# Block-sorted attention feeding a four-expert layer: another order for the first batch's stages and another chain for its sort weights

## The chip, the cores and the metric

The kernel runs on one core of a Trainium2 chip. Its metric is device time in microseconds (us), the median of the runs. The core has five engines with a queue each: TensorE (PE; its weight loads are listed apart as PEld), VectorE (DVE), ScalarE (ACT), GpSimd (POOL) and SyncE (SP). Transfers are issued by the queues of SP, POOL and ACT and carried out by sixteen DMA engines. Times inside a profile are microseconds from the start of its span.

## What is computed

Attention with sorted blocks, and then a dense mixture of four experts on its output. For 4 batches and 8 heads, a sequence of 768 is cut into 8 blocks of 96. An 8 x 8 matrix per head, normalised five times over, mixes the blocks of keys and values:

```python
P = sort_net
for _ in range(5):
    P = P - np.max(P, axis=-1, keepdims=True)
    P = np.exp(P)
    P = P / (np.sum(P, axis=-1, keepdims=True) + 1e-09)
    P = P / (np.sum(P, axis=-2, keepdims=True) + 1e-09)
k_sorted = einsum('bhij,bhjcd->bhicd', P, k_blocks)      # the same for v
scores = scale * q_block @ k_sorted_block.T              # each block against its own sorted block
x = softmax(scores) @ v_sorted_block                     # 3072 tokens x 512
p = domain_probs / (domain_probs.sum(-1) + 1e-09)
out = sum(p[:, e] * (np.maximum(x @ w1[e], 0) @ w2[e]) for e in range(4))   # w1: 512 x 1024
```

## The kernel before

The order is written out by hand: each engine runs its instructions in the order in which the code emits them (the pools only decide which buffer a tile gets), and waits on semaphores. There is no scheduler.

**The head.** All work of batch 0 up to the second layer of expert 0 is a hand-made list at the end of the function. The sort weights of all 32 heads are normalised together, as 32 rows of 64 numbers: five passes of one exp on ScalarE and six small VectorE instructions (L273 to L288), beside 84 and then 30 warm-up matmuls (`warm`). The result is spread (L293, half on VectorE, half on GpSimd), eight small matmuls (`r_half`, L305) turn it into a column per block, and `build_PI0` (L316) multiplies it with a mask into mixing blocks. Heads are taken in two quarters `qd` (heads 0 to 3 and 4 to 7), output blocks in two halves `hf`, and queries in four pieces `qq`, two in each half. The stages of the head are: `h_q`, transposed queries; `mix_half` and `mixed`, the mix of keys or values, and its copies; `h_w`, values transposed; `h_s`, scores and their exp; `h_a`, attention and its division; `h_x`, transposes into `xT`, the input of the experts. `group0` (L661) is expert 0's first layer, here mostly in groups of 192 columns, cut into two parts and put between the stages; `second_layer0` (L696) its second layer; it scales its result by that expert's weight.

**Buffers.** PSUM has two pools, `psM` and `psA`, of two tiles each. A new tile waits for the last reader of the buffer that it takes over.

**Loads.** GpSimd's queue issues, in this order: queries of the first half (both quarters), keys and values of quarter 0 and of quarter 1, expert 0's `w1` in two parts; then, when the sort weights are spread, queries of the second half, expert 0's `w2`, and `w1` and `w2` of experts 1 to 3; then queries, values and keys of batch 1. SyncE's queue writes the normalised domain weights to memory and reads them back spread over all partitions (`load_p`, tile `pb`). A load waits in its queue for the landing of the one that stands eight before it.

**After the head** come `second_layer0(0)`; the first layers of experts 1 and 2 for tokens 0 to 255 (`chunk_first`, L768, evacuated by VectorE, L774); VectorE's sums of their results (`h_sums`) and of expert 1's second weights (`weight_sums`, L727); expert 0 for the second half (`first_layer0`, evacuated by ScalarE, L674, and `second_layer0(1)`); and then, in chunks of 256 tokens, the rest of batch 0, with the attention of the next batch put into its slots by `PLANS`. Each unit of work calls a slot when it is done; `next_stages` puts the remaining head stages into the first slots.

Of the kernel before, what the change touches and what calls it, by code (L numbers as in the profile page):

```python
# [17 lines left out]
def kernel(  # L18
# [20 lines left out]
    P = 128  # L39
# [35 lines left out]
    sn = const.tile([GH, NB, NB], F32, name="sn")  # L75
    nc.sync.dma_start(sn[:], sort_net.rearrange("b h i j -> (b h) i j"))

# [17 lines left out]
    q0 = Tt[3].rearrange("p a f x -> p (a f x)").rearrange("p (f h r d) -> p f h r d", f=2, h=4, r=R)  # L95

# [44 lines left out]
    def load_half_queries(hf):  # L141
        for qd in range(2):
            nc.gpsimd.dma_start(
                q0[ds(64 * qd, 64), hf].rearrange("p h r d -> p h (r d)"), half_queries(qd, hf)
            )

    dummy = Hflat[:, ds(2 * NFC * 2 * P, P)]
# [12 lines left out]
    load_half_queries(0)  # L160
# [7 lines left out]
    load_natural(0, "v", 1)  # L168
    load_w1(0, 2)
# [10 lines left out]
    )  # L180

# [18 lines left out]
    vo = arena[:, ds(4 * NW + NQ + 4 * 4 * P, R * 4 * VW)].rearrange("p (r h w) -> p r h w", r=R, h=4)  # L200

# [16 lines left out]

    def spread_weights():
# [13 lines left out]
        pbs[(0, 0)] = load_p(0, 0)  # L233
# [11 lines left out]
    def warm(n):  # L245
        ps = psM.tile([P, 4, P], F32, tag="ps", name=f"ps_w_{state['n']}")
        state["n"] += 1
        for m in range(n):
            nc.tensor.matmul(ps[:, m % 4, :], dummy, dummy, start=True, stop=True)
# [3 lines left out]
    def h_q(qd, hf, copy):  # L253

        ps = psa([P, 2, R, 64], F16, f"ps_q_{qd}_{hf}")
# [12 lines left out]
    sn16 = const.tile([GH, NB, NB, CP], F16, name="sn16")  # L268
    warm(84)
    p_steps = spread_weights()  # L270
    nc.gpsimd.tensor_copy(ident6, ident[0:R, 0:R])
    for it in range(5):
        nc.scalar.activation(sn[:], sn[:], AF.Exp, bias=0.0, scale=1.0)  # L273
        if it == 4:
            for qd in range(2):
                h_q(qd, 0, nc.scalar.copy)
            warm(30)
        nc.vector.tensor_reduce(srow[:], sn[:], AX.X, ALU.add)
        nc.vector.reciprocal(srow[:], srow[:])
        nc.vector.tensor_tensor(sn[:], sn[:], srow[:].broadcast_to([GH, NB, NB]), ALU.mult)  # L280
        nc.vector.tensor_reduce(scol[:], sn[:].rearrange("p i j -> p j i"), AX.X, ALU.add)
        nc.vector.reciprocal(scol[:], scol[:])
        if it < 4:
            nc.vector.tensor_tensor(
                sn[:], sn[:],
                scol[:].rearrange("p j o -> p o j").broadcast_to([GH, NB, NB]),
                ALU.mult,
            )  # L288
            if it:
                next(p_steps)  # L290

    for a, eng in enumerate((nc.vector, nc.gpsimd)):
        eng.tensor_tensor(  # L293
            sn16[:, ds(a * HB, HB)],
            sn[:, ds(a * HB, HB)].rearrange("g i (j o) -> g i j o", o=1).broadcast_to([GH, HB, NB, CP]),
            scol[:].rearrange("g j (i o) -> g i j o", i=1).broadcast_to([GH, HB, NB, CP]),
            ALU.mult,
        )

    ps_R = psM.tile([P, 2, 512], F32, tag="ps", name="ps_R")  # L300
    Rv = ps_R[:, :, 0:HB * GH].rearrange("p a (i g) -> p a i g", g=GH)

    def r_half(a):
        for i in range(HB):
            nc.tensor.matmul(  # L305
                Rv[:, a, i, :], sn16[:, a * HB + i, :, :].rearrange("g j c -> g (j c)"),
                ident[0:GH, 0:GH], start=True, stop=True,
            )

# [32 lines left out]
    r_half(0)  # L342
# [970 lines left out]
    for qd in range(2):  # L1313
        for nm in ("v", "k"):
            load_natural(1, nm, qd)
# [65 lines left out]
```

## Time and profile before

| | |
|---|---|
| runs | 363.74 us median of 3 (362.68, 363.74, 364.23) |
| profiled execution | 363.03 us, its span 361.3 us |
| granted TensorE clock | 0.999 |
| busy: PE, PEld | 353.7 us (98%), 315.4 us (87%) |
| busy: VectorE, ScalarE, GpSimd | 276.6 (77%), 173.7 (48%), 134.2 (37%) |
| instructions | 10846, 4621 of them matmuls |
| moved by DMA | 40.47 MB |

A line of the timeline gives start, length, engine, source line, operation, the tile written and the tiles read, sizes and count, and in brackets the engine's idle time before it with what ended it. A group of matmuls is drawn as one line. The chain that ended last is followed back from the last instruction. Stretches give busy time of each engine in a window. Busy PE is not PE at its peak, since matmuls overlap and their ends are modelled.

### The profile page before, as it was taken

How to read it: one execution, taken by the hardware profiler on the slowest of the kernel's cores; microseconds unless marked ns; L12 is line 12 of the kernel's file. 1: busy time of each engine (PE TensorE's matmuls, PEld its weight loads, DVE VectorE, ACT ScalarE, POOL GpSimd, SP SyncE). 2: the span in 40 equal slices, each digit the busy share in tenths (PEclk: the TensorE clock that was granted, in tenths of full speed). 3: DMA queues.
4: the chain of work that ended last, by engine and by line, in shares of the span. 5: the costliest groups of instructions: out<-in, count | busy, mean ns of one | idle time of the engine just before them, and what ended most of it. 6: DMA issues, size and time to landing. Idle time of an engine off the chain costs nothing.

```text
span 361.3 us, 10846 instructions
## 1 busy us (share of the span) xinstructions
PE 353.7 (98%) x4621; PEld 315.4 (87%) x4621; DVE 276.6 (77%) x561; ACT 173.7 (48%) x306; POOL 134.2 (37%) x148
## 2 busy tenths in 40 slices
PE   8799999999999999999999999999999999999996
PEld 8686867888888888888889999999999998999995
DVE  5654798779788677868878978867679679587694
ACT  2665340451434355368937257175283481571750
POOL 8873010655022330000626318147065082180470
PEclk9999999999999999999999999999999999999999
DMA  7999999999999999935994310110302103102101
GB/s 100 204 206 230 209 210 199 200 192 177 189 167 146 201 121 172 166 80 72 170 200 78 60 60 2 60 60 3 94 27 47 73 3 60 61 2 62 58 11 49
DMA packets 71820, 40.47 MB, mean 112 GB/s; under 512 B 40534, under 2 KB 66524, under 8 KB 71772
## 3 DMA queue, kind: packets, MB, share of 16 engines
q0 software_dynamic: 36560, 19.93, 42.7%
q1 hardware_dynamic: 35068, 19.79, 27.8%
q8 instruction: 36, 0.59, 0.7%
q14 instruction: 12, 0.10, 0.1%
q10 hardware_dynamic: 144, 0.07, 0.1%
HBM read 42.00 MB, written 6.34 MB: 134 GB/s over the span
## 4 chain that ended last, share of the span: by engine, by line
PE 89%; DMA 6%; POOL 1%; DVE 1%; SPq 1%; ACT 1%; issue 1%; DVEq 0%; ACTq 0%; POOLq 0%
PE ps_Q L1141 24%; PE ps_h L768 16%; PE ps_p L753 10%; PE ps_X L1038 10%; PE ps_Z L1038 7%; PE ps_Q L1038 7%; DMA w<-in_moe_w_dram 4%; PE ps_h L661 3%; PE ps_o L696 3%; PE ps_p L803 2%; DMA vs<-arena 2%; PE ps_a L441 2%; PE ps_s L406 1%; PE ps_v L354 1%; SPq L368 1%; PE ps_k L387 1%
## 5 line engine op out<-in xcount | busy, mean ns | idle before, releaser
L1051 POOL TENSOR_TENSOR Hb<-tmp,pb 128x512 f16<-128x512 f32 x40 | 50.8, 1276 | 84.3 <-ACT tmp L1050 83.0
L768 PE MATMUL ps_h<-xT,w 128*128 128x256 f16 x576 | 67.8, 273 | 0.0
L768 PEld LDWEIGHTS <-w 128*128 128x128 f16 x576 | 55.1, 98 | 7.3
L1141 PEld LDWEIGHTS <-Hb 128*128 128x128 f16 x576 | 53.7, 98 | 5.6
L774 DVE SCALAR_TENSOR_TENSOR Hb<-ps_h,pb 128x1024 f16<-128x1024 f32 x36 | 44.0, 1223 | 17.9 <-PE ps_h L768 17.7
L1038 PEld LDWEIGHTS <-w 128*128 128x128 f16 x864 | 52.4, 98 | 1.2 <-issue 0.3
L1141 PE MATMUL ps_Q<-w,Hb 128*128 128x256 f16 (+1 forms) x352 | 43.4, 268 | 0.0
L1038 PEld LDWEIGHTS <-arena 128*128 128x128 f16 x552 | 33.4, 98 | 0.1
L413 ACT ACTIVATE ET<-ps_s 96x768 f16<-96x768 f32 x24 | 18.1, 802 | 26.5 <-PE ps_s L406 26.2
L1038 PE MATMUL ps_X<-kT,arena 128*128 128x128 f16 x384 | 29.3, 219 | 0.0
L1058 ACT COPY ps_X<-ps_Z 128x512 f32<-128x512 f32 x27 | 15.4, 570 | 28.7 <-PE ps_Z L1038 28.3
L396 ACT CAST kT<-ps_k 64x384 f16<-64x384 f32 x48 | 22.7, 474 | 12.8 <-PE ps_k L387 11.8
L1074 DVE TENSOR_TENSOR tmp<-ps_Q,tmp 128x512 f32<-128x512 f32 x26 | 18.0, 692 | 14.1 <-ACT tmp L1073 9.9
L121 POOL DMA_DIRECT2D arena<-in_q_dram x24 | 19.9, 837 | 19.1 <-DMA qT<-arena 18.2
L739 DVE TENSOR_TENSOR Sb<-Hb 128x512 f16<-128x512 f16 x45 | 26.3, 608 | 0.9 <-POOL Hb L1051 0.8
L1141 PE MATMUL ps_Q<-T,Hb 128*128 128x256 f16 x224 | 26.7, 273 | 0.0
L1050 ACT ACTIVATE tmp<-tmp 128x512 f32<-128x512 f32 x40 | 25.4, 634 | 1.2 <-DVE tmp L1074 1.0
L753 PEld LDWEIGHTS <-Hb 128*128 128x128 f16 x232 | 21.9, 98 | 3.0
L1141 PEld LDWEIGHTS <-Sb 128*128 128x128 f16 x240 | 22.1, 98 | 2.3
L1065 ACT COPY tmp<-ps_X 128x512 f32<-128x512 f32 x26 | 15.2, 586 | 13.0 <-PE ps_X L1038 13.0
L1051 POOL TENSOR_TENSOR Hb<-tmp7x,pb 128x512 f16<-128x512 f32 x14 | 19.0, 1355 | 5.7 <-ACT tmp7x L1050 5.7
L1044 DVE SCALAR_TENSOR_TENSOR Hb<-ps_X,pb 128x512 f16<-128x512 f32 x27 | 18.5, 684 | 2.7 <-PE ps_X L1038 2.7
(205 smaller groups left out, 652.8 us busy)
## 6 DMA issues: line engine op xcount, KB each, us to landing
w<-in_moe_w_dram POOLq DMA_DIRECT2D x7, 1024.0 KB, 27.7
pb<-p_dram SPq DMA_DIRECT2D x12, 512.0 KB, 5.5
arena<-in_k_dram POOLq DMA_DIRECT2D x8, 384.0 KB, 9.0
arena<-in_v_dram POOLq DMA_DIRECT2D x8, 384.0 KB, 9.0
vs<-arena SPq DMA_DIRECT2D x36, 66.0 KB, 5.6
arena<-in_q_dram POOLq DMA_DIRECT2D x24, 96.0 KB, 7.5
out_dram<-ob SPq DMA_DIRECT2D x9, 256.0 KB, 2.0
out_dram<-oa SPq DMA_DIRECT2D x8, 256.0 KB, 2.3
```

The source lines that it names most:

```text
L121: nc.gpsimd.dma_start(t[:, h // 2, :, h % 2, :], q[b, h].rearrange("(t p) d -> p t d", p=P))
L396: nc.scalar.copy(kT[ds(D * hh, D), r], pk[ds(D * r, D), hh].rearrange("p a (i c) -> p a i c", c=CP),)
L413: nc.scalar.activation(ETs[2 * (pr % 2) + hh][:, 0:S].rearrange("c (a x) -> c a x", a=2), pss[hh][0:BLK, :, 0:HS], AF.Exp, bias=0.0, scale ...
L739: tt(sm[0], blk(0, 1), blk(1, 1), ALU.add)
L753: nc.tensor.matmul(ps, lhs(e, f), Ts[e][rhs][:, f, :], start=(first and e == es[0] and f == 0), stop=(done and e == es[-1] and f == KH - 1 ...
L768: nc.tensor.matmul(ps[:, f, :], w1sb[e][:, kc, ds((4 * g + f) * P, P)], xT[:, kc, ds(2 * c * P, 2 * P)], start=(kc == 0), stop=(kc == NKC ...
L774: nc.vector.scalar_tensor_tensor(out=Hb[:, e, ds(4 * g, 4), :], in0=ps[:], scalar=0.0, op0=ALU.max, in1=pb[:, ds(e, 1), :].broadcast_to([P ...
L1038: nc.tensor.matmul(dst[:, ds(f * P, P)], a[lhs][:, k, ds(f * P, P)], t[rhs][:, k, :], start=(first and f == 0 and k == 0), stop=(f == KH - ...
L1044: nc.vector.scalar_tensor_tensor(out=Hb[:, e, ds(i * KH, KH), ds(j * P, P)], in0=src.rearrange("p (f x) -> p f x", f=KH), scalar=0.0, op0= ...
L1050: nc.scalar.activation(src, src, AF.Relu, bias=0.0, scale=1.0)
L1051: nc.gpsimd.tensor_tensor(Hb[:, e, ds(i * KH, KH), ds(j * P, P)], src.rearrange("p (f x) -> p f x", f=KH), pb[:, ds(e, 1), ds(j * P, P)].b ...
L1141: nc.tensor.matmul(ps, lhs(e, f), Ts[e][rhs][:, f, part], start=(first and e == 0 and f == 0), stop=(e == E - 1 and f == KH - 1), skip_gro ...
```

## The change

1. The sort weights of batch 0 (8 heads, 64 rows) get a chain of their own. Two loads (SP and ACT queues) bring them in; VectorE transposes them; each pass is an exp on ScalarE with the column factor as its scale, a f32 matmul with a block mask for the row sums, a reciprocal, a product that also sums the columns, and a reciprocal. The spread result goes through one matmul to the blocks. The other 24 heads follow in `later_steps`, one step in each slot after the head.
2. On GpSimd's queue the quarters of the queries are parted, the masks are made before the last of the quarter-1 loads, `w1` of expert 0 goes out after the memsets, and the second block build stands ahead of the second-half queries and expert 0's `w2`.
3. The list of the head's stages is in another order; expert 0's first layer comes in groups of 384 columns, after both query pieces of the first half. Warm-ups are 256 or 512 columns wide instead of 128.
4. The domain weights are written out in the head's start, and `pb` is asked for behind them. Expert 1's first layer for tokens 256 to 511 (`homes` puts it into expert 0's place) is done ahead of expert 3's first layer for tokens 0 to 255, with domain weights of its own, loaded by `load_p_one`.
5. `PLANS` moves entries of batch 1's attention by two to four slots.

```diff
+    HJ = H * NB
+    sn0, snT = early(HJ, 32), early(HJ, 32)
+    blocks8 = early(HJ, HJ)
+    e0, r0, a0, c0, c0r = [early(HJ, n) for n in (NB, NB, NB, 1, 1)]
+    sel8 = early(HJ, NB)
+    sel, spread0 = [early(HJ, n, F16) for n in (P, HJ)]
...
+    for n, eng in enumerate((nc.sync, nc.scalar)):
+        eng.dma_start(
+            sn0[ds(32 * n, 32)].rearrange("i (h j) -> i h j", j=NB),
+            bass.AP(tensor=sort_net.tensor, offset=n * H // 2 * NB * NB, ap=[[NB, 32], [NB * NB, H // 2], [1, NB]]),
+        )
+    nc.sync.dma_start(sn[:], sort_net.rearrange("b h i j -> (b h) i j"))
...
-    load_half_queries(0)
+    load_half_queries(0, [0])
+
+    nc.gpsimd.memset(blocks8, 1.0)
+    for base, m in ((0, 1), (NB - 1, -1)):
+        nc.gpsimd.affine_select(
+            out=blocks8, in_=blocks8, compare_op=ALU.is_ge, fill=0.0, base=base,
+            pattern=[[-m * NB, H], [0, NB]], channel_multiplier=m,
+        )
     load_natural(0, "k", 0)
...
     load_natural(0, "v", 0)
     load_natural(0, "k", 1)
-    load_natural(0, "v", 1)
-    load_w1(0, 2)
...
+    load_half_queries(0, [1])
+    load_natural(0, "v", 1)
...
+    load_w1(0, 2)
...
+    def load_p_one(b, c, e):
+
+        pb = Tt[3].rearrange("p a f x -> p (a f x)")[:, 0:4 * P].bitcast(F32)
+        nc.sync.dma_start(pb, p_dram[ds(e, 1), ds(b * S + 2 * c * P, 2 * P)].broadcast_to([P, 2 * P]))
         return pb
...
-        pbs[(0, 0)] = load_p(0, 0)
...
-    warm(84)
...
+    warm(7, 256)
+    nc.vector.transpose(snT, sn0)
     nc.gpsimd.tensor_copy(ident6, ident[0:R, 0:R])
+    now, scale = snT[:, 0:NB], 1.0
     for it in range(5):
-        nc.scalar.activation(sn[:], sn[:], AF.Exp, bias=0.0, scale=1.0)
-        if it == 4:
-            for qd in range(2):
-                h_q(qd, 0, nc.scalar.copy)
-            warm(30)
-        nc.vector.tensor_reduce(srow[:], sn[:], AX.X, ALU.add)
-        nc.vector.reciprocal(srow[:], srow[:])
-        nc.vector.tensor_tensor(sn[:], sn[:], srow[:].broadcast_to([GH, NB, NB]), ALU.mult)
-        nc.vector.tensor_reduce(scol[:], sn[:].rearrange("p i j -> p j i"), AX.X, ALU.add)
-        nc.vector.reciprocal(scol[:], scol[:])
+        nc.scalar.activation(e0, now, AF.Exp, bias=0.0, scale=scale)
+        sums = ps_c[0:HJ, 0, ds(it * NB, NB)]
+        nc.tensor.matmul(sums, blocks8, e0, start=True, stop=True)
         if it < 4:
-            nc.vector.tensor_tensor(
-                sn[:], sn[:],
-                scol[:].rearrange("p j o -> p o j").broadcast_to([GH, NB, NB]),
+            warm((4, 5, 7, 7)[it], 256)
+        else:
+            h_q(0, 0, nc.scalar.copy)
+        nc.vector.reciprocal(r0, sums)
+        nc.vector.scalar_tensor_tensor(
+            out=a0, in0=e0, scalar=1.0, op0=ALU.mult, in1=r0, op1=ALU.mult, accum_out=c0
+        )
+        nc.vector.reciprocal(c0r, c0)
+        now, scale = a0, c0r
+        if it in (1, 2):
+            pick_rows(it - 1)
+        if 0 < it < 4:
+            next(p_steps)
...
+    nc.vector.scalar_tensor_tensor(
+        out=spread0.rearrange("p (g i) -> p g i", i=NB), in0=a0.rearrange("p (o i) -> p o i", o=1).broadcast_to([HJ, H, NB]),
+        scalar=c0r, op0=ALU.mult, in1=blocks8.rearrange("p (g i) -> p g i", i=NB), op1=ALU.mult,
+    )
+    ps_R0 = psM.tile([P, 2, 512], F32, tag="ps", name="ps_R0")
+    R0 = ps_R0[:, 0, 0:HJ].rearrange("p (g i) -> p g i", i=NB)
+    nc.tensor.matmul(ps_R0[:, 0, 0:HJ], sel, spread0, start=True, stop=True)
+
+    def later_steps():
+
+        gp = nc.gpsimd
+        gp.memset(sn16[ds(GH, GH)], 0.0)
+        gp.memset(sn16[ds(2 * GH, 2 * GH)], 0.0)
+        for it in range(5):
+            nc.scalar.activation(sn[:], sn[:], AF.Exp, bias=0.0, scale=1.0)
+            yield
+            nc.vector.tensor_reduce(srow[:], sn[:], AX.X, ALU.add)
+            nc.vector.reciprocal(srow[:], srow[:])
+            gp.tensor_tensor(sn[:], sn[:], srow[:].broadcast_to([GH, NB, NB]), ALU.mult)
+            yield
+            nc.vector.tensor_reduce(scol[:], sn[:].rearrange("p i j -> p j i"), AX.X, ALU.add)
+            nc.vector.reciprocal(scol[:], scol[:])
+            if it < 4:
+                gp.tensor_tensor(
+                    sn[:], sn[:], scol[:].rearrange("p j o -> p o j").broadcast_to([GH, NB, NB]), ALU.mult,
+                )
+            yield
+        for a in range(2):
+            gp.tensor_tensor(
+                sn16[0:GH, ds(a * HB, HB)],
+                sn[:, ds(a * HB, HB)].rearrange("g i (j o) -> g i j o", o=1).broadcast_to([GH, HB, NB, CP]),
+                scol[:].rearrange("g j (i o) -> g i j o", i=1).broadcast_to([GH, HB, NB, CP]),
                 ALU.mult,
             )
-            if it:
-                next(p_steps)
-
-    for a, eng in enumerate((nc.vector, nc.gpsimd)):
-        eng.tensor_tensor(
-            sn16[:, ds(a * HB, HB)],
-            sn[:, ds(a * HB, HB)].rearrange("g i (j o) -> g i j o", o=1).broadcast_to([GH, HB, NB, CP]),
-            scol[:].rearrange("g j (i o) -> g i j o", i=1).broadcast_to([GH, HB, NB, CP]),
-            ALU.mult,
-        )
-
-    ps_R = psM.tile([P, 2, 512], F32, tag="ps", name="ps_R")
-    Rv = ps_R[:, :, 0:HB * GH].rearrange("p a (i g) -> p a i g", g=GH)
-
-    def r_half(a):
-        for i in range(HB):
+        for qd in range(2):
+            for nm in ("v", "k"):
+                load_natural(1, nm, qd)
+        for _ in range(3):
+            yield
+        ps = psa([P, 2, 512], F32, "ps_R")
+        Rv = ps[:, 0, 0:NB * GH].rearrange("p (i g) -> p i g", g=GH)
+        for i in range(NB):
             nc.tensor.matmul(
-                Rv[:, a, i, :], sn16[:, a * HB + i, :, :].rearrange("g j c -> g (j c)"),
-                ident[0:GH, 0:GH], start=True, stop=True,
-            )
-
+                Rv[:, i, :], sn16[:, i, :, :].rearrange("g j c -> g (j c)"), ident[:, 0:GH], start=True, stop=True,
+            )
+        nc.scalar.copy(Rs[:, H:GH, :].rearrange("p g i -> p i g"), Rv[:, :, H:GH])
+        builds(1)
...
-    r_half(0)
     for h0 in range(0, H, 4):
-        build_PI0(nc.vector, 0, h0, 4, Rv[:, 0, :, ds(h0, 4)].rearrange("p i g -> p g i"))
+        build_PI0(nc.vector, 0, h0, 4, R0[:, ds(h0, 4), 0:HB])
+    nc.scalar.copy(Rs[:, 0:H, :], R0)
+    build_PI0(nc.gpsimd, 1, 0, H, Rs[:, 0:H, HB:NB])
+    load_half_queries(1)
+    load_w2(0)
...
+    next(p_steps)
+    tile2 = lambda pool, nm: pool([P, 2, 512], F32, f"ps_{nm}")
+    mk0 = mix_half("k", 0, 0, psm, 2)
     mixed("k", 0, mk0, 0, 2, act)
+    mixed("k", 0, mk0, 2, 2, act)
     mv0 = mix_half("v", 0, 0, psa)
     mixed("v", 0, mv0, 0, 2, vec)
+    mixed("v", 0, mv0, 2, 2, vec)
     h_s(0, 0)
-    r_half(1)
-    mixed("k", 0, mk0, 2, 2, act)
-    vec(Rs.rearrange("p g (a i) -> p a g i", a=2), Rv.rearrange("p a i g -> p a g i"))
-    load_half_queries(1)
-    load_w2(0)
-    build_PI0(nc.gpsimd, 1, 0, H, Rs[:, 0:H, HB:NB])
+    ps_s01 = tile2(psm, "s01")
+    h_s(0, 1, ps_s01)
     h_w(0, vec, 0, 2, tails[("v", 0, 0)])
-    mixed("v", 0, mv0, 2, 2, vec)
     mk1 = mix_half("k", 1, 0, psm)
+    w01 = h_w(0, None, 2, 2, side(ps_s01))
+    w01(vec)
+    ps_a00 = tile2(psa, "a00")
+    h_a(0, 0, ps_a00)
     mixed("k", 1, mk1, 0, 2, act)
+    ps_a01 = tile2(psa, "a01")
+    h_a(0, 1, ps_a01)
+    h_q(1, 0, act, psm)
     mixed("k", 1, mk1, 2, 2, act)
-    ps_a00, ps_s10 = [psa([P, 2, 512], F32, f"ps_{n}") for n in ("a00", "s10")]
-    h_a(0, 0, ps_a00)
+    h_x(0, None, [0], ps_a00)
     mv1 = mix_half("v", 1, 0, psm)
-    mixed("v", 1, mv1, 0, 2, act)
+    ps_s10 = tile2(psm, "s10")
     h_s(1, 0, ps_s10)
-    ps_s01 = psm([P, 2, 512], F32, "ps_s01")
-    w01 = h_w(0, None, 2, 2, side(ps_s01))
-    h_x(0, act, [0], ps_a00)
+    copies.pop(0)(act)
+    mixed("v", 1, mv1, 0, 2, vec)
+    h_x(1, None, [0], ps_a01)
+    ps_s11 = tile2(psa, "s11")
+    h_s(1, 1, ps_s11)
+    copies.pop(0)(act)
+    mixed("v", 1, mv1, 2, 2, vec)
     h_w(1, vec, 0, 2, tails[("v", 1, 0)])
-    mixed("v", 1, mv1, 2, 2, act)
-    h_s(0, 1, ps_s01)
-    w01(act)
-    ps_a10 = psa([P, 2, 512], F32, "ps_a10")
-    keep_warm(ps_a10[:, 0, 0:P], 4)
+    w11 = h_w(1, None, 2, 2, side(ps_s11))
+    w11(vec)
+    h_k(0, 1, act, psm)
+    ps_a10 = tile2(psa, "a10")
+    keep_warm(ps_a10[:, 0, :], 1)
     h_a(1, 0, ps_a10)
-    next(p_steps)
-    group0(0, 1, 0, [0, 1])
-    ps_a01 = psa([P, 2, 512], F32, "ps_a01")
-    w11 = h_w(1, None, 2, 2, side(ps_a01))
+    ps_a11 = tile2(psa, "a11")
+    h_a(1, 1, ps_a11)
     h_x(0, act, [1], ps_a10)
-    h_a(0, 1, ps_a01)
-    w11(vec)
-    group0(0, 1, 1, [0, 1])
-    ps_s11 = psa([P, 2, 512], F32, "ps_s11")
-    h_s(1, 1, ps_s11)
-    evacuate00 = group0(0, 1, 0, [2, 3], True)
-    h_x(1, act, [0], ps_a01)
-    evacuate00()
-    group0(0, 1, 1, [2, 3])
-    h_a(1, 1, ps_s11)
-    h_k(0, 1, act)
-    group0(1, 1, 0, [0, 1])
-    h_x(1, vec, [1], ps_s11)
-    group0(1, 1, 1, [0, 1])
+    group0(0, 2, 0, [0, 1])
+    group0(0, 2, 1, [0, 1])
+    h_x(1, act, [1], ps_a11)
+    group0(0, 2, 0, [2, 3])
+    h_v(0, 1, vec)
+    group0(0, 2, 1, [2, 3])
     h_k(1, 1, vec)
-    group0(1, 1, 0, [2, 3])
-    group0(1, 1, 1, [2, 3])
+    group0(0, 2, 2)
+    h_v(1, 1, vec)
+    h_w(0, vec)
+    h_q(0, 1, vec)
+    group0(0, 2, 3)
+    h_w(1, vec)
+    h_q(1, 1, vec)
...
-    builds(1)
+    load_queries(1, range(2))
+    others = later_steps()
...
     def next_stages():
+        next(others, None)
         if later:
             for f, *args in later.pop(0):
                 f(*args)
 
-    h_v(0, 1, act)
-    h_q(0, 1, vec)
     second_layer0(0, next_stages)
-    load_queries(1, range(2))
-    for qd in range(2):
-        for nm in ("v", "k"):
-            load_natural(1, nm, qd)
+    pbs[(0, 0)] = load_p(0, 0)
+    pb_1 = load_p_one(0, 1, 1)
     chunk_first(0, 0, [1, 2], 1, next_stages)
     h_sums(1, 4)
     for w in range(1, 5):
...
     all_sums(1, nc.vector)
     first_layer0(2, 2, next_stages)
     sums2 = weight_sums(2, nc.vector)
-    second_layer0(1, lambda: next(sums2, None))
+
+    def with_sums():
+        next_stages()
+        next(sums2, None)
+
+    second_layer0(1, with_sums)
     sums0 = weight_sums(0, nc.vector)
+    homes[1] = 0
+    chunk_first(0, 1, [1], 1, next_stages, lambda e: pb_1.rearrange("p (o x) -> p o x", o=1))
+    homes.clear()
```

## The prediction

> Times are us from the span's start unless said otherwise.
>
> **What bounds the kernel now.** I read the page's chain first, then busy time by stretches, then the timeline of the head and of the stretch around 50. The chain:
>
> ```profile
> PE 89%; DMA 6%; POOL 1%; DVE 1%; SPq 1%; ACT 1%; issue 1%; DVEq 0%; ACTq 0%; POOLq 0%
> ```
>
> TensorE sets the end; only its idle time and its own work count. By stretches (columns: us; busy PE, PEld, DVE, ACT, POOL; clock; DMA share; GB/s):
>
> ```profile
> 0.00:12.00 12.00, 9.66 (x166) 9.32 (x166) 7.44 (x34) 3.93 (x8) 9.41 (x29) 1.00 0.90 123
> 12.00:19.50 7.50, 6.00 (x172) 5.04 (x168) 4.62 (x11) 5.25 (x11) 6.56 (x10) 1.00 1.20 209
> 19.50:28.00 8.50, 8.43 (x166) 7.70 (x168) 4.06 (x9) 5.13 (x10) 6.95 (x8) 1.00 1.26 208
> ...
> 47.00:57.00 10.00, 9.99 (x55) 5.18 (x53) 9.74 (x18) 3.25 (x4) 0.74 (x1) 1.00 1.18 209
> ```
>
> The first 12 us are the sort chain under warm-up matmuls. 12 to 19.5 holds 1.5 us of PE idle, 19.5 to 28 nearly none. From 47 to 57 VectorE is as full as PE. In the head's timeline these rows give the anchors:
>
> ```profile
> 12.66 0.57 PE L483 MATMUL ps_mk<-Sb,arena 128*64 128x64 f16 x24
> 14.19 0.81 ACT L544 ACTIVATE ET<-ps_s 96x768 f16<-96x768 f32 x1 [0.44 <-PE ps_s L538]
> 16.13 0.57 PE L483 MATMUL ps_mv<-Sb,arena 128*64 128x64 f16 x24 [0.35 <-DMA arena<-in_v_dram]
> 19.57 0.83 PE L661 MATMUL ps_h<-xT,w 128*128 128x192 f16 x8 [0.83 <-DMA w<-in_moe_w_dram]
> 28.78 1.04 PE L696 MATMUL ps_o<-w,Hb 128*128 128x512 f16 x4
> ```
>
> The first key mix starts at 12.66, the second layer of expert 0 at 28.78. Two loads are waited for (values 16.13, w1 19.57); w2_0, issued at 13.89 and 14.8 us under way, lands at 28.7, just in time. Around 50:
>
> ```profile
> 50.33 0.69 DVE L727 TENSOR_TENSOR T<-w 128x1024 f16<-128x1024 f16 x1
> ...
> 52.50 0.69 DVE L727 TENSOR_TENSOR T<-w,T 128x1024 f16<-128x1024 f16 x1
> 53.11 0.68 DVE L727 TENSOR_TENSOR T<-w 128x1024 f16<-128x1024 f16 x1
> ```
>
> ```profile
> 50.85 0.81 ACT L674 ACTIVATE Hb<-ps_h 128x768 f16<-128x768 f32 x1 [0.55 <-PE ps_h L661]
> 52.09 0.81 ACT L674 ACTIVATE Hb<-ps_h 128x768 f16<-128x768 f32 x1 [0.43 <-PE ps_h L661]
> ```
>
> VectorE runs without a gap from 46.72 to 58 and is behind PE: expert 1's weight sums end at 53.1, when PE (second layer from 51.90) is already six matmuls in. ScalarE delivers the last hidden group at 52.9, just before it is read.
>
> **The skill.** "TensorE: Matmul & The Clock Gate", section on the array's architecture, calls ScalarE and VectorE strict FIFO: a waiting instruction holds all behind it. The trace agrees: a hidden group whose matmuls ended at 22.74 was evacuated only at 23.33, behind a copy at 22.95. The same page (What's actually happening) says the clock opens after about 3.4 us of activity; here matmul spacing halves near 5.5, after 4.4 us of warm-ups. "DMA: Bandwidth & Descriptors" (Issuing engines are not separate DMA queues) says all queues share the engines; the pb load issued at 26.29 took 11.7 us against a median of 5.5.
>
> **The change, part by part.**
> *Sort chain.* A pass takes 1.76 now (exps at 4.27, 6.04, 7.80). New pass: exp 0.26, f32 matmul 0.35 (nearest row: the f32 transpose, weights 0.13 + 0.22), reciprocal 0.19, product with running sum 0.25, reciprocal 0.19, handovers 0.3 (0.04 to 0.11 each in the trace) = 1.54. Bounds: 1.35 with a shorter matmul, 1.75 if the 256-column warm-ups ahead of it still run at the slow clock. The first exp starts at 2.85 (data at 2.5 as now, though in 256 short rows from two queues; ScalarE issues one, 0.4, and loads its table, 1.28, till then; one 32-block transpose 0.2 to 0.3, which no row shows). Five passes end at 10.55; product 0.25, matmul 0.3, first block build 0.37, handovers 0.15: key mix at 11.6 (10.8 to 12.3), 1.1 earlier than 12.66. The sums of the domain weights and the selector (0.16 to 0.28 each) fit into VectorE's wait of about 0.7 per pass.
>
> *Head order.* From the key mix, m, the new order is one thread through ScalarE, because the second half's query copy moves from 9.7 (idle ScalarE) into the middle. Durations from this trace: mix 0.57, two key copies 0.96, two exps 1.62, handover and the copy of R 0.2: m+3.35. The second value transpose writes into the score tile and so waits for that exp: transpose 0.39, copy 0.42, attention 0.41, query transposes 0.56, query copy 0.73, handovers 0.35: m+6.2. Key copy 0.48, scores 0.35, exp 0.81, xT copy 0.48 (the next score tile reuses its bank), scores 0.34, exp 0.81, value transposes 0.39, handovers 0.35: m+10.2. Mix 0.5, warm-up 0.22, attention 0.41, reciprocal and product 0.89, transposes 0.34, handovers 0.15: m+12.7. Four then four 384-column matmuls (0.163 each, from 32 in 5.2): 1.3 covers the other xT; its transposes and copy 0.85: m+14.8. What is left is PE work: 24 such matmuls 3.9, three mixes 1.5, two value transposes 0.9, two query transposes 1.0, waits for copies 0.3: m+22.4 = 34.0. Now the second layer starts at 28.78 but has 1.9 of that still to do (one mix, one query half, two value transposes at 0.46 to 0.5), so the like point is 30.7: 3.3 late. The 384-column form saves about 0.6 against the eight groups of 192 (0.66 to 0.83 each); that is inside. I take 3.0, for hops counted twice; bounds 0 (PE is never held, only w2_0's landing) and 4.5 (cold PE in addition).
>
> *Loads.* On GpSimd's queue the block mask (about 0.9, nearest rows 0.27 and 0.30) and then the small masks and memsets come before later issues: w1's two go out near 10 instead of 6.27, and w2_0 behind the second block build near 15 instead of 13.89. The queue is then still moving keys and values, which land till 16.1, so both are hidden by that backlog; without it each would cost its delay, 1 to 4. Bytes ahead of w1 and w2_0 are the same; keys of the second half land about 1 earlier, queries near 14, before ScalarE asks for them. The weights of the first 768 tokens and pb now leave at about 11 and 17 instead of 19.96 and 26.29; pb's 512 KB at 205 GB/s are 2.5, of which w2_0 already bore 0.5: it lands at about 30.7, under the 34.0 of PE, hidden (cost 1 to 2 if PE were early). pb for one expert, 128 KB, 0.6, is hidden by 5 us of later slack. The SyncE queue's query transpose now stands behind it, but its own data land near 62 either way.
>
> *The other 24 heads' chain* is moved into slots of the second layer and what follows: five exps on ScalarE, 20 small VectorE instructions (0.19 to 0.26), ten GpSimd products. Up to 46 VectorE has room; one pair sits before the product that the last xT transposes need (they started at 44.32 as soon as it ended): 0.4. The fourth and fifth pass sit behind expert 1's weight sums on the full VectorE, and the fifth exp sits on ScalarE ahead of the last hidden group's evacuation. From 53.1: reduce and reciprocal 0.45, GpSimd product 0.3 (nearest: 128x64 0.35, 128x32 0.24), reduce and reciprocal 0.5, product 0.3, exp 0.26, evacuation 0.81, handovers 0.25: 56.0. PE needs that group at 51.90 + 6 x 0.216 = 53.2. Stall 2.8; bounds 2.3 (products at 0.15) and 3.4. Behind it wait VectorE's two last ops, then the output scaling (57.3 to 58.0), which PE needs at 58.2: nothing more. The products sn16 and four loads of batch 1 wait on GpSimd too, to about 62; the values then land by 66 to 70, read near 72.
>
> *Moved at no price:* R for the other heads, 8 small matmuls, 0.3 more in a full stretch (before, in a head with gaps). Expert 1's layer ahead: 32 matmuls (3.5) change place; it gives expert 3's loads 3.5 more, which PE, late already, does not need. PLANS shifts: the slots lost are those of that expert; PE idle from 57 to 187 is under 0.4 now, so nothing is won and up to 1 could be lost.
>
> Sum: 3.0 + 2.8 + 0.4 + 0.3 = 6.5. The profiled execution took 363.03 (span 361.3): 369.5. The runs' median is 0.7 above it: about 370.
>
> **Rivals.** *Only one of the two costs appears* (+2.5 to +4, 366 to 368): for it, PE could fill the thread better than I count, as it does from 19.5 on now. *Nothing is felt* (within 0.5%): PE held only by w2_0 at 30.7, and the fifth exp in time; against it the full VectorE. *Faster:* the head is paced by loads alone. Then the second layer starts with w2_0; if pb does not delay it (28.7), that is 2.0 early: 361.7, at best 360. It decides if the thread from the key mix takes under 19 us, not 22.4, and the fifth exp's group stalls PE by less than the gain. For it: two DMA waits in the head now. *Slow clock:* the warm-ups have gaps; if the clock stays at half until the mixes, passes take 1.75 and the mixes 1 to 2 more: 372 to 374.
>
> **How the numbers follow.** Both costs 0.46, one of them 0.25, nothing felt 0.10, faster 0.11, slow clock on top 0.08. 0.5% is 1.8 us, about what a measurement can tell. Faster 0.11, same 0.10, slower 0.79. Likeliest 370 (its own range 367.5 to 372.5); the range 363 to 373 leaves out the faster case and the worst of the slow clock.
>
> **What would show it.** Key mix near 11.6 (right), second layer near 34 with ScalarE between its tiles all the way (right), or near 30 with a wait for w (wrong). In the second layer of the second half a PE wait of 2 to 3 us on ScalarE, with the small exp waiting on GpSimd (right). Without both, the prediction is wrong.

## The result, and the profile after

The changed kernel takes 377.05 us (median of 4 runs, 375.30 to 378.22), the kernel before 363.57 (362.68 to 364.23): ratio 1.0369, 95% interval 1.0322 to 1.0415. It is slower by 13.5 us where 6.4 were forecast, and lies above the forecast range. The profiled execution took 377.06, its span 375.3, 14.0 longer than before.

The chain of work that ended last, of the changed kernel:

```profile
PE 84%; DVE 7%; DMA 4%; ACT 2%; issue 1%; SPq 1%; POOL 0%; DVEq 0%; ACTq 0%; POOLq 0%
```

TensorE lost five points of the chain, and VectorE won six. Busy time by stretches, columns as before (us; busy PE, PEld, DVE, ACT, POOL; clock; DMA share; GB/s):

```profile
0.00:12.00 12.00, 9.36 (x74) 5.60 (x75) 5.02 (x30) 3.49 (x7) 9.22 (x31) 1.00 0.89 125
12.00:19.50 7.50, 5.46 (x176) 4.70 (x176) 4.91 (x12) 4.96 (x10) 6.30 (x10) 0.98 1.22 209
19.50:28.00 8.50, 7.16 (x73) 4.87 (x73) 2.54 (x6) 2.85 (x6) 2.92 (x4) 0.50 1.25 210
...
57.00:71.00 14.00, 11.40 (x67) 6.11 (x65) 10.45 (x21) 3.03 (x5) 8.22 (x11) 0.88 0.79 103
```

The news is in the clock column. From 19.5 to 28 TensorE runs at half clock, where it had 1.00 before; from 57 to 71 it idles for 2.6 and has half clock again for a part. In the trace's record of the clock, these stretches run from 19.25 to 29.49 and from 63.62 to 67.04. The record begins only when the clock first opens, at 9.0 here and at 5.4 in the kernel before; ahead of that the column reads 1.00, although the matmuls are spaced as at half clock (seven warm-ups of 256 columns take 1.68 from 6.67 on, and seven take 1.13 from 8.59 on). The anchors of the head, in the timeline:

```profile
11.91 0.57 PE L564 MATMUL ps_mk<-Sb,arena 128*64 128x64 f16 x24
17.74 0.67 PE L564 MATMUL ps_mv<-Sb,arena 128*64 128x64 f16 x24 [0.60 <-ACT Sb L297]
19.96 0.51 PE L619 MATMUL ps_s<-Sb,kT 64*128 64x96 f16 x8 [0.99 <-ACT xT L665]
25.02 2.76 PE L746 MATMUL ps_h<-xT,w 128*128 128x384 f16 x8
37.42 1.04 PE L781 MATMUL ps_o<-w,Hb 128*128 128x512 f16 x4
```

The key mix starts at 11.91. TensorE then waits for ScalarE's copies (the query copy at 17.7, the xT copy at 20), and eight matmuls of 384 columns take 2.76, 0.33 each, where one took 0.163 before. The second layer of expert 0 starts at 37.42. And around 60:

```profile
58.79 1.46 PE L781 MATMUL ps_o<-w,Hb 128*128 128x512 f16 x6
61.84 0.26 ACT L354 ACTIVATE sn<-sn 32x64 f32<-32x64 f32 x1 [3.29 <-POOL sn L363]
62.01 0.78 ACT L759 ACTIVATE Hb<-ps_h 128x768 f16<-128x768 f32 x1
62.85 4.88 PE L781 MATMUL ps_o<-w,Hb 128*128 128x512 f16 x14 [2.60 <-ACT Hb L759]
67.56 0.36 PE L382 MATMUL ps_R<-ident,sn 128*128 128x32 f16 x8
```

The fifth exponential of the later chain waits for GpSimd till 61.84 and holds the last hidden group's evacuation behind it; TensorE waits 2.60. The 14 matmuls that follow take 4.7, and 3.0 at the full clock (0.216 each).

Start of like work in both kernels (us):

| | before | after | later by |
|---|---|---|---|
| first key mix | 12.66 | 11.91 | -0.75 |
| first layers of experts 1 and 2 (all head work of TensorE's first half done) | 37.97 | 44.78 | 6.8 |
| expert 0, first layer, second half of the tokens | 46.52 | 53.41 | 6.9 |
| expert 0, second layer, second half | 51.90 | 58.79 | 6.9 |
| the first layer after it | 57.08 | 68.63 | 11.6 |
| end of the span | 361.3 | 375.3 | 14.0 |

So 6.8 are lost in the head, 4.7 in the second layer of the second half, 2.4 behind it.

### The profile page after: what moved, and what is told of

It is laid out like the page before. It is cut to its first block, busy times and chain, and to the rows that moved or that the text cites. A ratio compares the mean times of both kernels' runs of the same rounds, so it can differ in the third digit from the quotient of the medians.

```text
span 375.3 us, 10682 instructions
## 1 busy us (share of the span) xinstructions
PE 359.2 (96%) x4507; PEld 311.9 (83%) x4507; DVE 281.2 (75%) x579; ACT 173.1 (46%) x308; POOL 140.2 (37%) x163
## 4 chain that ended last, share of the span: by engine, by line
PE 84%; DVE 7%; DMA 4%; ACT 2%; issue 1%; SPq 1%; POOL 0%; DVEq 0%; ACTq 0%; POOLq 0%
PE ps_Q L1229 23%; PE ps_h L856 15%; PE ps_X L1126 9%; PE ps_p L840 8%; PE ps_Q L1126 6%; PE ps_Z L1126 6%; PE ps_o L781 3%; PE ps_p L891 2%; DMA vs<-arena 2%; PE ps_h L746 2%; DMA w<-arena 2%; PE ps_a L522 1%; PE ps_s L487 1%; PE ps_warm L283 1%; PE ps_v L435 1%
## 5 line engine op out<-in xcount | busy, mean ns | idle before, releaser
L862 DVE SCALAR_TENSOR_TENSOR Hb<-ps_h,pb 128x1024 f16<-128x1024 f32 x34 | 41.5, 1223 | 16.9 <-PE ps_h L856 16.7
L826 DVE TENSOR_TENSOR Sb<-Hb 128x512 f16<-128x512 f16 x45 | 27.6, 637 | 0.0
```

What stands on the lines that cost most here:

```text
L826: tt(sm[0], blk(0, 1), blk(1, 1), ALU.add)
L862: nc.vector.scalar_tensor_tensor(out=Hb[:, homes.get(e, e), ds(4 * g, 4), :], in0=ps[:], scalar=0.0, op0=ALU.max, in1=weights(e).broadcast ...
```

## The experiments

Each ran beside the kernel before on the same chip; the ratio is to those runs. The changed kernel itself stands at 1.0369.

### The head: does idle TensorE time close the clock gate?

*c1_head_warm*, the changed kernel with warm-ups in two waits of the head:

```diff
     h_x(0, None, [0], ps_a00)
+    keep_warm(ps_a00[:, 1, :], 3)
...
     h_x(1, None, [0], ps_a01)
+    keep_warm(ps_a01[:, 1, :], 4)
```

> The changed kernel with seven more 512-column warm-up matmuls: three behind the first tokens' transposes (0.6 us of idle there, near 17.1) and four behind the second tokens' transposes (1.0 of idle, near 19). Theory that the two idle stretches close the clock gate: the granted clock stays at 1.00 from 12 to 30, the matmuls between 19.5 and 29 run at 0.163 per 384 columns and not 0.32, the second layer of expert 0 starts at about 34.0 and not 37.5, and the whole takes 377.0 - 3.5 = 373.5. Rival, the head is held by the thread through ScalarE alone and the half clock only fills waits: the clock stays at 1.00, the second layer starts no more than 1 earlier, 376 to 377. Second rival, the gate closes for another reason than idle time: clock and time as in the changed kernel, or 0.5 longer.

Measured: 375.54, ratio 1.0347 (1.0304 to 1.0390). Its stretches and its second layer:

```profile
12.00:19.50 7.50, 6.56 (x182) 5.00 (x181) 4.86 (x13) 4.40 (x9) 5.87 (x9) 1.00 1.22 206
19.50:28.00 8.50, 6.49 (x107) 4.18 (x105) 3.11 (x9) 4.44 (x8) 3.33 (x4) 1.00 1.27 220
```

```profile
24.40 1.47 PE L746 MATMUL ps_h<-xT,w 128*128 128x384 f16 x8
34.97 1.04 PE L781 MATMUL ps_o<-w,Hb 128*128 128x512 f16 x4
```

The clock stays at 1.00, eight 384-column matmuls take 1.47 and not 2.76. From the key mix (12.39 in this execution) to the second layer it is 22.6, where the changed kernel takes 25.5: the half clock cost 2.9 in that execution, and the thread without it is nearly the forecast's 22.4. TensorE is 2.5 earlier at the second layer and 2.8 at the end. The medians are only 1.5 apart, since the runs of this kernel spread from 374.4 to 377.3 (what spreads them is taken up below), so the size is read from the trace, not from the total. All profiled executions with the new head, of this run and of those below, agree. The eight without these warm-ups (the changed kernel, c2, c3, d1, d2, d3, e2 and f3) went to half clock in the head for 6.8 to 13.7 us and took 25.1 to 27.7 for this thread; the three with them (c1, e3 and f2) never did, and took 22.6. In d2 the clock had first opened at the same time as in c1, 10.5, so the moment of opening is not what spared c1.

*c4_old_head*: the changed kernel with the list of head stages (and the first slots) of the kernel before, the query copy of quarter 1 behind the key copies.

> The changed kernel with the head stages of the kernel before: their order, the groups of 192 columns, the value mixes and query transposes of the second half left to the second layer's slots. The short sort chain, the loads, the wider warm-ups, the later chain and expert 1 ahead stay as changed. Theory that the new order of stages costs the head 6.8 of its lateness: the second layer starts at about 28.8 - 0.8 = 28.0 to 29, 377.0 - 6.8 = 370.2, with the stall of 2.6 near 55. Rival, the loads (w2 of expert 0 behind the second block build) or the queries' later load hold the old order too: the second layer starts at 31 or later, 373 or more.

Measured: 370.75, ratio 1.0234 (1.0176 to 1.0292), 6.3 under the changed kernel; nearly all that the table gives to the head. In its profiled execution, the slowest of the four at 374.8, the rival showed as well: TensorE waited 2.37 for expert 0's second weights, till 32.61. This execution had half clock three times, for 3.4 each. Two of the others (371.3 and 370.2) were granted 1.000 on average, so in them no half clock followed the stall near 60, which this program has too.

*f3_more_warm*: `warm((5, 6, 10, 12)[it], 256)` in the sort chain, for 4, 5, 7, 7.

> The changed kernel with 5, 6, 10 and 12 warm-up matmuls behind the row sums of the first four passes and not 4, 5, 7 and 7, so that TensorE has hardly a gap in the sort chain. Theory that the small row-sum matmuls and gaps keep the clock gate shut until 9 to 15: matmul spacing halves by 9 in every pass order, the key mix starts at 11.6 to 12.0, and the head is as before behind it; 376.5. Rival, the opening only depends on when matmuls began, and the added warm-ups delay each row sum by up to 0.3: key mix at 12.5 or later, 377 to 378.

Measured: 378.01, ratio 1.0387 (1.0329 to 1.0444), key mix at 12.81. The theory falls: more warm-ups delay the chain and do not bring the full clock sooner (it opens at 9.04, for 9.01 in the changed kernel). In the other profiled executions with the changed chain the key mix started between 11.8 and 12.7, and but for f1, whose passes were slower, it follows the opening of the clock: 11.8 to 11.9 where the clock opened at 8.2 to 9.0, 12.1 to 12.4 for 9.8 to 10.5, and 12.7 where it opened only at 14.7 to 16.4, behind the mix. With warm-ups without a break it opened at 5.4 (the kernel before) and 5.9 (e4). Why it opens so differently under one and the same chain is not shown; the last section has what the record of the clock says.

### The second layer: is it the exponential, and what does the half clock add?

*c3_stall_warm*, warm-ups put into the stall itself:

```diff
                 if fc == KH - 1:
                     slot()
+                if (hf, t, fc) == (1, 0, 5):
+                    keep_warm(po[:, 1, :], 12)
```

> The changed kernel with twelve 512-column warm-up matmuls (2.6 us) put into the stall of the second layer, ahead of the matmul that waits. The stall itself stays. Theory that the idle stretch closes the clock gate for the next 3.5 us: 14 matmuls behind it take 3.0 and not 4.9, 377.0 - 1.8 = 375.2. Rival, the clock falls for another reason (the heavy matmuls before it): no change, 377.

Measured: 375.02, ratio 1.0342 (1.0303 to 1.0381).

```profile
59.87 2.75 PE L550 MATMUL ps_o<-Hb 128*128 128x512 f16 x12
62.64 3.19 PE L781 MATMUL ps_o<-w,Hb 128*128 128x512 f16 x14
```

From the first of the 14 matmuls behind the stall to the matmuls of R (the eight small ones that turn the other heads' sort weights into columns, at 65.67 here) it is 3.0 and not 4.7. In the changed kernel's execution the wait of 2.6 costs 1.7 more than its own length, by the clock alone.

*c2_exp5_after*: `next_stages` skips the chain once, in its 13th call, so that the fifth exponential stands behind the last evacuation.

> The changed kernel with one slot left out of the later sort chain, so that its fifth exponential stands behind the last hidden group of tokens 768 to 1535 on ScalarE, and not ahead of it. Theory (the stall of the fourth step, and the half clock that follows it): no wait of 2.6 in the second layer, no half clock from 63.5 to 67 (1.75), together 4.35: 372.7. Rival, the stall is only moved: the matmuls of R and the scaled outputs come late instead, since the fifth pass now ends about 1 later, and the time is 375 to 377.

Measured: 376.09, ratio 1.0346 (1.0301 to 1.0390). The rival is right. TensorE no longer waits for ScalarE, but 1.4 for the scaled outputs (VectorE) and, in the middle of R's matmuls, 1.2 for a product of GpSimd that they read. No half clock follows these waits. From the start of the second half to the next first layer it is 8.5, for 9.8 in the changed kernel and 5.2 before. (Its head ran longer at half clock, till about 35, so the total says little.)

### Taking the chain out of the way, and a wait that takes its place

*d1_two_passes* (`for it in (0, 4)`: three of the five passes of the other 24 heads left out, which computes something else, to see the place without them) and *d2_early_chain*, all five passes but three steps in two slots:

```diff
     def next_stages():
+        held["n"] += 1
         next(others, None)
+        if held["n"] < 10 and held["n"] % 2:
+            next(others, None)
```

> The changed kernel, but the other 24 heads get two sort passes and not five (three are left out, so this computes something else); every step of that chain then stands nine slots earlier. Theory that the late fifth exponential and what hangs on it (R, the half clock) is the loss around 60: no wait of 2.6, no half clock behind it, the stretch from the first matmul of the second layer's second half to the next first layer takes 5.2 to 5.5 and not 9.8, and batch 1's loads leave near 55 and not 66. 377.0 - 4.4 = 372.6; and if the late loads of batch 1 are what loses another 2 to 2.5 after 70, 370.3. Rival, VectorE is so full there that the second layer is held anyway: 9 in that stretch, 376.

> The changed kernel with all five passes, but three steps of the later chain in every two slots from the start of the second layer, so that the last step stands in the tenth slot, before expert 1's weight sums. Theory: as with two passes, no stall near 60, batch 1's loads leave near 56, 370.5 to 372.6, less what the denser chain costs before 53: 0 to 1. Rival, a chain step now takes longer than a slot and half, VectorE and ScalarE wait for it in order, and the stall is spread over the slots before 53: 375 to 377, with the wait on VectorE's copies between 40 and 53.

Measured: 375.12, ratio 1.0353 (1.0317 to 1.0388), and 381.51, ratio 1.0504 (1.0452 to 1.0555). With the fifth exponential long done, TensorE now waits for VectorE's scaled outputs, 2.3 in the first and 5.0 in the second. The second is slower than the changed kernel, its profiled execution by 4.3: 2.3 arise in the head, where it had half clock for 13.7 us and not 10.2, and 2.1 in this stretch (11.9 for 9.8). *d4_old_head_early* puts the same early chain under the old head stages:

> The head stages of the kernel before and the earlier steps of the later chain together, on the changed kernel. If the two costs (head 6.3 by the earlier run, second layer 4.4) add up: 377.0 - 6.3 - 4.4 = 366.3, and 364.5 if batch 1's earlier loads bring their 2. Rival, one hides the other (a head that ends earlier runs into the load of expert 0's second weights, and the chain's slots come earlier than its data): 369 to 371.

Measured: 374.82, ratio 1.0339 (1.0293 to 1.0386): the old head's gain is eaten. Its timeline shows by what:

```profile
55.92 0.69 DVE L812 TENSOR_TENSOR T<-w 128x1024 f16<-128x1024 f16 x1
56.64 4.91 DVE L812 TENSOR_TENSOR T<-w,T 128x1024 f16<-128x1024 f16 x1
61.48 0.68 DVE L812 TENSOR_TENSOR T<-w 128x1024 f16<-128x1024 f16 x1
```

```profile
56.92 1.08 POOL L413 TENSOR_TENSOR arena<-maskv,Rs 128x512 f16<-128x512 f16 x1
57.93 1.07 POOL L405 TENSOR_TENSOR arena<-maskk,Rs 128x512 f16<-128x512 f16 x1
58.94 1.06 POOL L413 TENSOR_TENSOR arena<-maskv,Rs 128x512 f16<-128x512 f16 x1
59.94 1.05 POOL L405 TENSOR_TENSOR arena<-maskk,Rs 128x512 f16<-128x512 f16 x1
```

One weight sum of 0.69 takes 4.91: it ends 0.6 after GpSimd's four products (the block matrices of batch 1, L405 and L413) have ended. With the early chain they fall beside expert 1's weight sums. The Trainium skill names a cause in "SBUF — State Buffer" (SBUF: two separate sides): a VectorE instruction with two SBUF inputs and a GpSimd instruction that reads SBUF share a port pair, which one holds for its whole instruction while the other fully blocks. Both kinds stand here. By that section the one that starts first holds the ports; in this trace the sum is recorded as starting 0.28 ahead of the first product, and it was the one that waited.

*e4_before_builds_moved* tests it in the kernel before, with `builds(1)` moved from behind `load_w2(3)` to behind `first_layer0(2, 2, next_stages)` and nothing else:

> The kernel before with one thing moved: GpSimd's four products that build batch 1's block matrices stand behind the first layer of tokens 768 to 1535 and so beside expert 1's weight sums on VectorE, not near 24 to 28. Theory that the two engines hold each other up: VectorE's sums there take up to 1.27 and 4.9 each, the second layer waits 3 to 5 for the scaled outputs, 366 to 368. Rival, the products are harmless there: 363, within 0.5%.

Measured: 366.98, ratio 1.0126 (1.0081 to 1.0171), 4.2 slower.

```profile
51.07 5.13 DVE L727 TENSOR_TENSOR w<-w 128x1024 f16<-128x1024 f16 x1
...
51.59 1.06 POOL L335 TENSOR_TENSOR arena<-maskv,Rs 128x512 f16<-128x512 f16 x1
...
52.60 1.04 POOL L327 TENSOR_TENSOR arena<-maskk,Rs 128x512 f16<-128x512 f16 x1
53.60 1.04 POOL L335 TENSOR_TENSOR arena<-maskv,Rs 128x512 f16<-128x512 f16 x1
54.61 1.04 POOL L327 TENSOR_TENSOR arena<-maskk,Rs 128x512 f16<-128x512 f16 x1
...
58.97 0.38 PE L696 MATMUL ps_o<-w,Hb 128*128 128x512 f16 x1 [3.44 <-DVE room L705]
```

The sum at 51.07 ends 0.6 behind the fourth product, and TensorE waits 3.44 for a scaled output that stands behind it.

*e1_old_head_late_builds* and *e3_new_head_fixed* (the latter with the new head and c1's warm-ups) write `builds(1)` behind `second_layer0(1, with_sums)`:

> The run with the old head stages and the early chain, with one thing moved: GpSimd's four products that build batch 1's block matrices stand behind the second layer's second half, and no longer beside expert 1's weight sums. Theory that VectorE and GpSimd hold each other up (a 512-element sum took 1.27 and not 0.41, one of 1024 took 4.91 and not 0.69, while GpSimd's products ran): the wait of 5.0 for the scaled outputs goes, 374.8 - 5 = 370 or, with the half clock behind it, 368. Rival, the wait comes from the denser chain on VectorE: no more than 1 faster.

> The changed kernel with its own head stages and three things: the warm-ups that hold the clock in the head, the early chain, and the builds of batch 1 behind the second layer. If the head's half clock (2.5 to 3) and the stall near 60 with its half clock (4.4) are both undone: 377.0 - 7 = 370. Rival, the denser chain holds the head's followers: 373 to 375, with waits between 40 and 53.

Measured: 374.77, ratio 1.0326 (1.0304 to 1.0349), and 376.23, ratio 1.0369 (1.0349 to 1.0390): nothing won, and the waits of 5.0 are still there. The edit moved nothing in time: no other instruction of GpSimd's queue stands between the old place and the new, and so the products ran from 59.2 and 59.1 on all the same. *f1_old_head_held* and *f2_new_head_held* add a true dependency:

```diff
     second_layer0(1, with_sums)
+    nc.gpsimd.tensor_copy(srow[:, 0, :], oaccs[R - 1][0:GH, 0:1])
     builds(1)
```

> As the run with the old head stages, the early chain and the builds written later, but GpSimd is now truly held: before the four products it copies one column of the last scaled output of the second layer. In the run before, the products still ran at 59.2, since nothing in GpSimd's own queue stood in their way. Theory of the shared port: the wait of 4.9 goes, the stretch from the second layer's second half to the next first layer takes 5.5 to 6.5 and not 11.9, 374.8 - 6 = 368.8. Rival, the chain's other work on VectorE and GpSimd keeps the scaled outputs late: 373 or more.

> The same one-line hold on the run with the new head stages, the warm-ups in the head and the early chain. Theory: 376.2 - 6 = 370.2, so that of the 13.5 lost about 3.5 are the half clock of the head and 4 the stretch near 60, and the rest is the longer thread of the head (3.3) and transfers. Rival, as for the old head: 374 or more.

Measured: 369.41, ratio 1.0135 (1.0097 to 1.0173), and 371.09, ratio 1.0216 (1.0151 to 1.0280). VectorE and GpSimd of f1:

```profile
58.95 0.69 DVE L811 TENSOR_TENSOR T<-w,T 128x1024 f16<-128x1024 f16 x1
59.56 0.68 DVE L811 TENSOR_TENSOR T<-w 128x1024 f16<-128x1024 f16 x1
60.16 0.74 DVE L789 TENSOR_SCALAR room<-ps_o,p_sb 128x512 f32<-128x512 f32 x1
```

```profile
64.22 0.18 POOL L1417 COPY srow<-room 32x1 f32<-32x1 f32 x1 [4.98 <-DVE room L789]
64.36 1.04 POOL L412 TENSOR_TENSOR arena<-maskv,Rs 128x512 f16<-128x512 f16 x1
```

The same sum takes 0.69, the stretch is 6.3 for 11.9, and one line brings 5 us and more (f1 against e1, f2 against e3). f2, the changed kernel without the head's half clock and without the stall, is about 6 us under the changed kernel, and still 2.2% above the kernel before.

### What is lost behind 70, and the loads

*d3_mid_loads*: batch 1's four loads of keys and values in the 8th, 9th, 11th and 12th call of `next_stages`, not behind the chain.

> The changed kernel with batch 1's four loads of keys and values issued in the 8th, 9th, 11th and 12th slot (near 47 to 56) and not behind the later chain (66 to 69). The stall near 60 stays. Theory that late loads of batch 1 push the transfers behind them and cost 2 to 2.5 after 70: no waits for transfers near 128 and 209, 375.0. Rival, these waits have another cause (expert 1's layer ahead, the plan's slots): 377.

Measured: 378.68, ratio 1.0425 (1.0372 to 1.0477). The wait for values near 136 grew to 1.6, so the late loads are not its cause. The run is slower because two of the loads stood among the chain's products on GpSimd: the fifth exponential went from 61.84 to 62.66 (0.4 of it a later head), the stall from 2.60 to 3.01, and the 14 matmuls behind it ran longer at half clock (5.9).

*e2_no_ahead*: without expert 1's layer ahead, with the plan of the kernel before.

> The changed kernel without expert 1's first layer ahead and with the plan of the kernel before for batch 0 (its first 18 entries). Theory that this part costs the 2.4 lost after 70 (waits for transfers near 128 and 209): 377.0 - 2.4 = 374.6. Rival, the part is neutral, as the prediction has it (0 to 1), and the loss comes from the late loads or from the lateness itself: 376 to 377.

Measured: 376.91, ratio 1.0388 (1.0361 to 1.0415). That part is neutral.

*g1_w2_first*: f1 with `load_w2(0)` ahead of GpSimd's second block build.

> The run with the old head stages, the early chain and the held builds, with the load of expert 0's second weights issued ahead of GpSimd's second block build and of the second half's queries (near 11, not 15). Theory that the changed order of loads was hidden only while TensorE was late: the wait of 2.35 for these weights near 30 goes, and so does the half clock behind it, 369.4 - 3 = 366.4. Rival, the load only takes bandwidth from the first weights and the values, and the waits for these grow by as much: 369.

Measured: 369.55, ratio 1.0171 (1.0148 to 1.0195). What TensorE waits for in the first 45 us, in f1 and then in g1 (total, times, longest):

```profile
PE ps_o L780 <- DMA w<-in_moe_w_dram: 2.4, 1, 2.4
```

```profile
PE ps_q L294 <- DMA T<-in_q_dram: 1.5, 1, 1.5
PE ps_mv L563 <- DMA arena<-in_v_dram: 0.7, 1, 0.7
```

The wait for the weights goes and one for the second half's queries comes. The rival is right: from 12 to 32 the transfers move 215 GB/s in f1 and 212 in g1, and the order only chooses which of them is late.

No run beat the kernel before. The best of those with the short sort chain, f1, has the old head and loses 1.35% all the same.

## Why the prediction was wrong

*What was right.* Slower, for the two reasons named as costs. The first step's pass of 1.54 is 1.52 in the trace (exps at 2.98, 4.49, 6.01, 7.53), though the fifth came after 1.92, and the key mix at 11.91 for 11.6. The pass held although TensorE was at half clock until 9.0, for which the forecast had 1.75. The second step's thread of 22.4 is 22.6 where the clock holds (12.39 to 34.97, and 12.11 to 34.70 in f2). The fourth step's stall of 2.8 is 2.60, in the place and by the order named (exponential, then evacuation). R is 0.2 for 0.3; expert 1 ahead and the shifted plan cost nothing that e2 could find.

*Where it failed: one rule, in two steps.* The second step set "cold PE in addition" as a bound of 4.5, and the rival of a slow clock sought it only in the warm-ups, with 0.08. The clock did close, later: TensorE was busy for 5.46 of 7.5 us from 12 to 19.5, the clock closed at 19.25, 0.3 into a gap of 0.99 and with no longer gap than 0.60 since the key mix, and 10.2 us at half followed. That is 2.9 in the head (c1). The fourth step priced the stall at its length and the clock behind it at nothing; the half clock adds 1.7 (c3), or 1.85 by the table's difference (9.84 - 5.18 - 2.60 - 0.2). An account of the difference in the profiled execution, against the span of 367.8 that the sum gave:

| term | forecast | measured |
|---|---|---|
| head, to the first layers of experts 1 and 2 | 3.0 | 6.8: half clock 2.9; the longer thread, less the earlier key mix, 3.9 |
| wait for the product of the last xT | 0.4 | 0.3 (at 51.48), of which 0.1 shows in the start times |
| second layer of the second half, R with it | 3.1 | 4.7: stall 2.6, half clock about 1.85, R 0.2 |
| behind it | 0 | 2.4 |

*The last row is half open.* In the trace these are waits for transfers: 1.1 for values near 136, 1.1 for the weight sums of the last chunks near 209, the rest in small pieces. The fifth step (expert 1 ahead, the plan) is not their cause (e2), nor are the late loads of batch 1 (d3). They come and go: from the next first layer to the end the loss is 0.3 in c2's execution, 3.3 in f3's, and 1.2 to 2.2 in most. As c1's runs differ by 3 us at nearly the same mean clock (0.994 to 1.00), they are the likeliest source of its spread, but no run isolates it. In c4 the spread goes with the clock instead: the slowest run has 0.985, the others 0.994 to 1.000.

*The third step was right by luck.* The forecast hid expert 0's loads behind the queue's backlog. They were hidden because TensorE was late by more: under the old head (c4, f1) it waited 2.4 for the second weights.

*A rival misjudged.* "Only one of the two costs" would have been my way to mend the kernel: move the fifth exponential, win 2.8. Moving it (c2) won 1.3 of 4.7 in that stretch, and moving the whole chain (d2) lost 2.1 more there, because GpSimd's products came along and blocked VectorE. The forecast looked at GpSimd's queue for what stands behind what, and not for what runs beside VectorE's sums.

## What to carry to other kernels

Price a stall of TensorE as its length, and set beside it the risk that the matmuls behind it run at half clock; in a thin stretch count all the idle time, not only the longest gap. Which gap closes the clock differed between executions, so one trace is not enough to say. A few warm-up matmuls inside a wait cost nothing (c1, c3), but ahead of the work that is waited for they delay it (f3). Before moving work in time, look at what VectorE and GpSimd do at the new place: here a VectorE sum of SBUF tiles stood still while GpSimd's products of SBUF tiles ran. And to move an instruction in time, give it a dependency; another place in the program means nothing where its own queue is empty.

## What the hardware showed that was not expected

The Trainium skill, "TensorE: Matmul & The Clock Gate" (HAM oscillation — how this bites in real kernels), asks for no idle gaps above about 3.4 us. The measurements differ from it on both sides. In the changed kernel the clock went to half with no gap over 0.99, and again after a single one of 2.60; in e4 TensorE waited 3.44, and the clock stayed at 1.00. The measurement decides. The changed kernel, and then e4, by the record of the clock:

```profile
15.84:19.25 3.41, 2.41 (x72) 2.08 (x72) 2.46 (x7) 1.70 (x3) 2.85 (x6) 1.00 1.17 210
19.25:29.49 10.24, 8.08 (x76) 5.28 (x76) 2.76 (x7) 3.58 (x7) 3.17 (x4) 0.50 1.22 212
60.21:63.62 3.41, 0.81 (x5) 0.41 (x5) 1.59 (x8) 0.95 (x2) 0.88 (x3) 1.00 0.67 47
63.62:67.04 3.42, 3.42 (x10) 1.22 (x8) 3.38 (x5) 0.00 (x0) 3.39 (x3) 0.50 0.29 58
```

```profile
53.71:57.12 3.41, 1.82 (x9) 0.72 (x8) 3.34 (x3) 0.00 (x0) 1.94 (x2) 1.00 1.22 207
57.12:60.53 3.41, 1.56 (x8) 0.73 (x8) 3.32 (x6) 0.00 (x0) 0.00 (x0) 1.00 1.60 188
```

In the 18 traces every half-clock stretch, but for the one at the very end, lasts 3.41 us or two, three or four times that, and so do all the times from one change of the clock to the next. This fits a clock that is set once in 3.41 us, at moments that differ between executions. The gap of 2.60 fell whole into one such window (0.81 of 3.41 us busy), and the longer gap of e4 into two (1.82 and 1.56 busy).

The busy share alone does not decide. In g1 the window from 15.84 to 19.25 is as busy as in the changed kernel, 2.41 us, and the clock stayed at 1.00. What differs is how much of TensorE's array the matmuls use. An estimate from the two traces: columns streamed, times the share of the array's 128 rows and 128 columns in use, come to 2480 in the changed kernel and 3180 in g1, where 8100 would fill the window (0.216 for 512). No run varies this alone, so what the clock counts stays open.

One VectorE sum waited for four GpSimd products in a row (5.13 for 0.69), and not just for one. VectorE's evacuations from PSUM were not touched: 1.23 each at 70.58 and 72.33 in the changed kernel, while the same products ran on GpSimd from 69.42 on, for 1.23 elsewhere.
